# Seven-product form for the last batch and the state reads, with weight sums and early state reads moved, in a fused attention and feed-forward kernel

## The chip, the cores and the metric

The kernel runs on one core of one Trainium2 chip. The metric is the device time of one execution in microseconds (us). "PE" is the matmul engine, "DVE" the vector engine, "ACT" the scalar engine, "POOL" the general engine, "SP" the engine that here only issues DMAs.

## The reference, cut to what matters

```python
# x (8, 8, 512, 64), state (8, 8, 32, 64): batch, head, token, width
scores = scale * x @ state.T ;  a  = softmax(scores)  ; xread = a  @ state   # 512 rows a batch
scores2 = scale * state @ x.T ; a2 = softmax(scores2) ; sread = a2 @ x      # 32 rows a batch
X = concat([xread, sread], tokens), heads side by side    # (8 * 544, 512)
h = X @ w_in                                               # 512 -> 2048
g = s * relu(h)**2 + b
out = g @ w_out                                            # 2048 -> 512
```

The last matrix product (mm2) is what the change rewrites. The 32 state-read rows of all eight batches are collected and treated as one block of 256 tokens, named `sr`, at the very end.

## The kernel before

Weights and activations are fp16, sums fp32. In step s of the main loop the kernel makes the hidden values of batch s (`mm1_x`, 16 pieces f of 128 hidden units) and, between them, the mm2 of batch s-1. For batches 1 to 6 mm2 is the seven-product form of a 2x2 block product (Strassen's idea in Winograd's form): 7 products of quarter size instead of 8, paid for by sums of token blocks (`token_sum`) and of weight blocks (`weight_sums`) on DVE, and by evictions that add partial results. Batches 0 and 7 and `sr` use the plain form:

```python
def mm2_part(key, rr, f0, f1):           # plain: 128 tokens x 512 outputs, 16 matmuls of 512 columns
    ...
def mm2_halves(key, rr):                 # the last 128 tokens of batch 7: two halves of 256 columns
    for n0 in (0, DM // 2):
        ops = psO.tile([P, DM // 2], FP32, tag="o", ...)      # a PSUM bank of its own for each half
        for f in range(NKF):
            mm(ops, G[key, f][:, P * rr : P * rr + P], wof(f)[:, n0:n1], ...)
        evac(ops, key, rr, n0, n1, [(nc.sync, 0, P, x_dst(key, rr)[:, n0:n1])])

# fast_items(b): seven products in banks A (p1, p2), B (p6, p7, p4), C (p5, p3);
# every bank holds two token blocks [P, 2, 256]; 112 matmuls of 256 columns
```

The parts of the main loop that the change touches, and the end:

```python
if s in fast:                            # fast = batches 1 to 6
    if f in (7, 11):
        with tc.issue_after(G["last"]): token_sum(s, 3, f // 8)
    if f in (11, 12, 13): token_sum(s, (1, 2, 4)[f - 11], 0)
    ...
if (s == 1 and f in (5, 7, 9, 14)) or (s == 2 and f in (2, 3, 4, 6)):
    with tc.issue_after(G["last"]): sums.pop(0)()       # one of eight weight sums
# in step 2: state reads of batches 0, 1 and 2, one after the other
at(10, lambda: att_V(s)); at(11, lambda: att_srT(s))
at(12, lambda: att_V(0)); at(12, lambda: att_V(1))
at(13, lambda: att_srT(0)); at(13, lambda: att_srT(1))
...
for f in range(4, NKF):                  # the end
    mm1_sr(f)
    if todo: unit(todo.pop(0))           # batch 7, plain form
for u in todo + sr_units: unit(u)        # sr, plain form; stores on POOL
mm2_halves(last_b, SCH - 1)              # stores on SP
```

PE, SP and POOL run in the order written; the order of DVE and ACT is chosen by the scheduler that builds the program. Output buffers (`osb`) come from a ring of three.

The softmax here doesn't subtract the row's maximum and nothing guards it: scores larger than these inputs give would overflow.

## Time and profile before

| | before |
|---|---|
| time, median of 4 runs | 220.55 us (220.32 to 220.77) |
| span of the profiled run | 218.9 us |
| PE's last matmul ends | 215.2 us |
| last store issued | 215.8 us |

The first line is from the busy table of the page (busy us, share, number of instructions), the second the shares by engine of the chain of work that ended last.

```profile
PE 207.2 (95%) x1916; PEld 125.9 (58%) x1916; DVE 145.3 (66%) x261; ACT 131.6 (60%) x224; POOL 41.5 (19%) x72
...
PE 73%; DVE 13%; DMA 8%; ACT 2%; POOL 1%; issue 1%; SPq 0%
```

PE is the bound: to gain time one must take matmuls away, or waits of PE. A matmul of 512 columns shows as 379 ns busy and one of 256 as 273, but these ends overlap: the starts lie 216 and 109 ns apart, and those are the costs to count with. PE's waits between 48 and 83 us of the kernel before (who waited for whom: total us, times, longest):

```profile
PE srT L68 <- DVE sr L293: 1.0, 2, 0.8
PE oB L68 <- DVE u L477: 0.6, 1, 0.6
PE oA L68 <- DVE osb L372: 0.5, 1, 0.5
PE oA L68 <- DVE qa L474: 0.3, 1, 0.3
PE oB L68 <- DVE s L429: 0.2, 1, 0.2
```

This view counts from the modelled end of a matmul. Counted from start to start, less the distance that the same matmuls keep elsewhere (216 ns after one of 512 columns, 109 after one of 256), the same waits are 1.32, 0.75, 0.58, 0.47 and 0.32 us: 3.4 us, all for DVE. The timeline of DVE just then (start, us, engine, line, operation, out and in) shows why:

```profile
49.49 0.69 DVE L330 TENSOR_TENSOR g<-r 128x1024 f16<-128x1024 f16 x1 [0.32 <-ACT r L324]
50.09 0.69 DVE L423 TENSOR_TENSOR s<-g 128x1024 f16<-128x1024 f16 x1
50.70 0.69 DVE L427 TENSOR_TENSOR s<-g,g 128x1024 f16<-128x1024 f16 x1
51.30 0.75 DVE L372 SCALAR_TENSOR_TENSOR osb<-o,s_bc,bias_bc 128x512 f32<-128x512 f32 x1
51.96 0.68 DVE L429 TENSOR_TENSOR s<-s,g 128x1024 f16<-128x1024 f16 x1
```

No idle time stands in brackets after the first line: DVE is full, one instruction each 0.60 to 0.66 us, and the eviction `osb` that PE waits for stands behind two token sums. Just before, there was room. A window of the same trace, 38 to 49 us (length, then busy us of PE, PEld, DVE, ACT, POOL): DVE worked 6.13 us of 11.

```profile
38.00:49.00 11.00, 11.00 (x93) 4.48 (x92) 6.13 (x12) 8.83 (x16) 2.54 (x4) 1.00 0.95 170
```

The end of the kernel before, from the timeline:

```profile
211.57 3.66 PE L68 MATMUL o<-wo,g 128*128 128x256 f16 x32
...
213.52 0.49 DVE L372 SCALAR_TENSOR_TENSOR osb<-o,s_bc,bias_bc 128x256 f32<-128x256 f32 x1 [0.99 <-PE o L68]
214.03 2.11 SPq L374 DMA_DIRECT2D out_dram<-osb  x2
215.26 0.48 DVE L372 SCALAR_TENSOR_TENSOR osb<-o,s_bc,bias_bc 128x256 f32<-128x256 f32 x1 [1.26 <-PE o L68]
```

This is a good end: the last eviction 0.03 us after PE, and the last store issued at 215.77, 0.54 us after PE's end. From PE's end to the end of the span it takes 3.7 us.

### The profile page before, as it was taken

The page shows a single profiled execution, that of the slowest core. Times are in us where ns is not written, and L with a number is a line of the kernel's source. Part 1 is how long each engine was busy: PE and PEld are TensorE (multiplying, and loading weights), DVE is VectorE, ACT ScalarE, POOL GpSimd, SP SyncE. Part 2 cuts the span into 40 slices and gives each one's busy share as a digit, 9 for nine tenths or more (in the row PEclk, how much of TensorE's full clock was granted, in tenths as well). Part 3 has the DMA queues.
Part 4 walks back from the last instruction along what each step waited for, and adds up shares of the span by engine and source line. Part 5 has one row for each costly group of instructions (what it writes and reads, how often), then busy time and mean ns, then how long its engine had stood idle before and what let it go on. Part 6 is the DMA issues. An engine that isn't in the chain of part 4 may idle for free.

```text
span 218.9 us, 4633 instructions
## 1 busy us (share of the span) xinstructions
PE 207.2 (95%) x1916; PEld 125.9 (58%) x1916; DVE 145.3 (66%) x261; ACT 131.6 (60%) x224; POOL 41.5 (19%) x72
## 2 busy tenths in 40 slices
PE   7897989999989999999999999999999999999993
PEld 2423333345556566667656765676667677655552
DVE  1686737739997778569856985699569955522221
ACT  3685654789488537965697569746974555332200
POOL 5960010403010310212021201120111011120042
PEclk9999999999999999999999999999999999999999
DMA  6999995999901890991199119211311111121123
GB/s 187 220 205 203 206 190 98 137 204 154 143 12 39 185 195 10 167 171 48 48 126 208 58 49 165 78 48 51 96 51 48 51 48 48 51 96 48 51 48 96
DMA packets 38776, 23.72 MB, mean 108 GB/s; under 512 B 24100, under 2 KB 36644, under 8 KB 38756
## 3 DMA queue, kind: packets, MB, share of 16 engines
q0 software_dynamic: 15792, 16.72, 39.4%
q1 hardware_dynamic: 22548, 6.62, 17.3%
q8 instruction: 15, 0.25, 0.5%
q10 hardware_dynamic: 416, 0.10, 0.2%
q14 instruction: 5, 0.04, 0.1%
HBM read 17.33 MB, written 8.91 MB: 120 GB/s over the span
## 4 chain that ended last, share of the span: by engine, by line
PE 73%; DVE 13%; DMA 8%; ACT 2%; POOL 1%; issue 1%; SPq 0%
PE h L68 18%; PE oB L68 14%; PE o L68 11%; PE oC L68 9%; PE oA L68 7%; DMA xn<-in_x_dram 5%; PE Mps L68 4%; PE h_sr L68 3%; PE o_sr L68 3%; DVE g L330 3%; DMA xf<-in_x_dram 3%; DVE s L429 1%; DVE s L427 1%; PE D L68 1%; DVE osb L464 1%; PE V L68 1%
## 5 line engine op out<-in xcount | busy, mean ns | idle before, releaser
L324 ACT ACTIVATE r<-h 128x512 f16<-128x512 f32 x126 | 74.1, 599 | 53.0 <-PE h L68 51.2
L68 PE MATMUL h<-a,M 128*128 128x512 f16 x256 | 74.9, 379 | 1.2 <-DVE a L242 0.7
L330 DVE TENSOR_TENSOR g<-r 128x1024 f16<-128x1024 f16 x64 | 44.2, 691 | 22.1 <-ACT r L324 21.9
L68 PEld LDWEIGHTS <-g 128*128 128x128 f16 x432 | 40.9, 98 | 22.4 <-issue 4.3
L68 PEld LDWEIGHTS <-s 128*128 128x128 f16 x384 | 36.0, 98 | 17.2 <-issue 4.6
L466 POOL DMA_DIRECT2D out_dram<-osb x24 | 16.2, 675 | 119.1 <-DVE osb L464 110.2
L68 PE MATMUL o<-wo,g 128*128 128x512 f16 (+1 forms) x144 | 32.3, 356 | 0.0
L68 PEld LDWEIGHTS <-M 128*128 128x128 f16 x256 | 24.6, 98 | 10.5 <-issue 2.5
L68 PE MATMUL oB<-wd,s 128*128 128x256 f16 x192 | 27.9, 273 | 1.0 <-DVE u L477 0.6
L68 PE MATMUL oA<-wo,g 128*128 128x256 f16 x192 | 27.2, 272 | 0.8 <-DVE osb L372 0.5
L266 ACT CAST M<-Mps 128x1024 f16<-128x1024 f32 x26 | 26.3, 1011 | 0.6
L68 PE MATMUL Mps<-wi,stT 64*32 64x512 f16 x256 | 13.3, 385 | 1.2 <-DMA wi<-in_moe_w_in_dram 1.2
L68 PE MATMUL oC<-wd,s 128*128 128x256 f16 x96 | 14.3, 273 | 0.0
L68 PEld LDWEIGHTS <-stT 64*32 64x32 f16 x384 | 5.3, 90 | 14.7 <-issue 10.3
L68 PE MATMUL oB<-wd,g 128*128 128x256 f16 x96 | 13.6, 273 | 0.0
L68 PE MATMUL oC<-wo,s 128*128 128x256 f16 x96 | 13.4, 273 | 0.0
L324 ACT ACTIVATE r_sr<-h_sr 128x256 f16<-128x256 f32 x16 | 6.1, 382 | 10.7 <-PE h_sr L68 10.7
L242 DVE TENSOR_TENSOR a<-E,R 128x1024 f16<-128x1024 f16 (+1 forms) x9 | 5.7, 632 | 7.2 <-ACT R L241 7.2
L464 DVE SCALAR_TENSOR_TENSOR osb<-oC,s_bc,u 128x512 f32<-128x512 f32 x12 | 9.0, 748 | 2.0 <-PE oC L68 2.0
L240 ACT ACTIVATE L<-D 128x1024 f32<-128x1024 f32 (+1 forms) x9 | 8.3, 925 | 2.5 <-PE D L68 2.5
L217 ACT ACTIVATE E<-T 128x512 f16<-128x512 f32 x16 | 9.4, 596 | 0.7 <-PE T L68 0.7
L330 DVE TENSOR_TENSOR g_sr<-r_sr 128x512 f16<-128x512 f16 x8 | 3.4, 424 | 9.5 <-ACT r_sr L324 9.5
(80 smaller groups left out, 201.8 us busy)
## 6 DMA issues: line engine op xcount, KB each, us to landing
out_dram<-osb POOLq DMA_DIRECT2D x31, 256.0 KB, 2.5
xn<-in_x_dram POOLq DMA_DIRECT2D x7, 512.0 KB, 9.5
wi<-in_moe_w_in_dram POOLq DMA_DIRECT2D x4, 512.0 KB, 9.0
wo<-in_moe_w_out_dram POOLq DMA_DIRECT2D x4, 512.0 KB, 16.2
xf<-in_x_dram SPq DMA_DIRECT2D x2, 512.0 KB, 4.9
out_dram<-osb_sr POOLq DMA_DIRECT2D x8, 64.0 KB, 2.0
out_dram<-osb SPq DMA_DIRECT2D x2, 128.0 KB
st<-in_state_dram POOLq DMA_DIRECT2D x1, 192.0 KB, 19.6
```

The source lines that it names most:

```text
L68: return nc.tensor.matmul(out, lhsT, rhs, start=start, stop=stop, tile_position=tp, is_transpose=is_transpose, skip_group_check=True,)
L217: nc.scalar.activation(a["E"][:, g, :].rearrange("p (m t) -> p m t", m=2), T[:, :, 256 * i : 256 * i + 256], AF.Exp, scale=scale, accum_ou ...
L240: nc.scalar.activation(a["L"][:, sl], Dps, AF.Ln)
L242: nc.vector.tensor_mul(a["a4"][:, sl], a["E"][:, sl], a["R"][:, sl])
L266: nc.scalar.copy(dst, ps)
L324: nc.scalar.activation(r16[:, f % 2], hps, AF.Relu)
L330: nc.vector.tensor_mul(gt[:, f % 4 - 1 : f % 4 + 1], r16, r16)
L427: nc.vector.tensor_add(o, a21, a22)
L429: nc.vector.tensor_sub(o, SQ[b, 1, j], a11)
L464: nc.vector.scalar_tensor_tensor(osb, acc[bank], s_bc, add, ALU.mult, ALU.add)
L466: nc.gpsimd.dma_start(dst[j][:, :, n0 : n0 + NH], osb)
```

## The change

Its intent: save matmul columns in batch 7 and `sr` by the seven-product form as well, and take DVE work out of the crowded stretch. To keep the tail short, the last product of batch 7 is run one token block after the other, each evicted and stored by itself. The core of the diff, cut:

```diff
     def put(bank, add, j, n0):
-        osb = opool.tile([P, 2, NH], FP32, ..., tag="osb")
+        osb = opool.tile([P, ni, NH], FP32, ..., tag="osb")        # ni = 1 for "sr", else 2
         nc.vector.scalar_tensor_tensor(osb, acc[bank], s_bc, add, ALU.mult, ALU.add)
+        if b == "sr":
+            for i in range(4):
+                dst = out_BSn[4 * j + i, S:ST, n0 : n0 + NH]
+                nc.sync.dma_start(dst, osb[Ns * i : Ns * i + Ns, 0])   # 32 rows each
+            return
         ...
+    def put_last(i):                                               # last product of batch 7, block i
+        osb = opool.tile([P, NH], FP32, ..., tag="osb")
+        nc.vector.scalar_tensor_tensor(osb, acc["C"][:, i], s_bc, kept["u2"][:, i], ...)
+        nc.sync.dma_start(dst[0][i][:, NH:DM], osb)
 ...
+    if b == last_b: out += [(3, k, i) for i in range(ni) for k in range(8)]   # block by block
+    else:           out += [(3, k, i) for k in range(8) for i in range(ni)]
 ...
-    if f in (7, 11):
+    if f in ((7, 9) if s == 1 else (7, 11)):
         with tc.issue_after(G["last"]): token_sum(s, 3, f // 8)
+    if s == 1 and f in (12, 13, 14):
+        with tc.issue_after(G["last"]): token_sum(s, (1, 2, 4)[f - 12], 0)
 ...
-    if (s == 1 and f in (5, 7, 9, 14)) or (s == 2 and f in (2, 3, 4, 6)):
+    if (s == 1 and 4 <= f < 11) or (s == 2 and f == 4):            # weight sums
 ...
+    at(13, lambda: att_V(0))                                       # in step 1
+    at(1, lambda: att_srT(0)); at(8, lambda: att_V(1)); at(10, lambda: att_srT(1))   # in step 2
-    at(12, lambda: att_V(0)); at(12, lambda: att_V(1)); at(13, ...); at(13, ...)
 ...                                                               # the end
+    for f in range(4, NKF):
+        mm1_sr(f)
+        ...token sums of "sr"...
+        go(rest, 5)                      # batch 7's products; from f = 12 on also 2 of sr's
+    go(rest, 12); go(rows, 4); go(rest, 8); go(rows, 44)
+    go(rest, 16)                         # last product of batch 7
```

(`tc.issue_after(G["last"])` ties the place of a sum in DVE's order to a matmul; `at(f, ...)` puts a piece of work into step s behind piece f; `V` is the product that makes a batch's state reads, `srT` their transposition on PE. PSUM is the memory in which matmuls add up, in banks; a tile is a buffer that the program asks for.) The state reads use banks of other PSUM pools for A, B and C; their partial results take a free buffer of the inputs.

More of the change, by code (lines that the diff above doesn't have):

```diff
@@ L418, in token_sum @@
     def token_sum(b, i, j):
-        SQ[b, i, j] = spool.tile([P, 4, TH], FP16, name=f"s{i}_{b}_{j}", tag="s")
+        n = (B * Ns if b == "sr" else S) // 2
+        SQ[b, i, j] = spool.tile([P, 4, n], FP16, name=f"s{i}_{b}_{j}", tag="s")
         o = SQ[b, i, j]
-        a11, a21 = G4[b, j][:, :, 0:TH], G4[b, j][:, :, TH:S]
+        a11, a21 = G4[b, j][:, :, 0:n], G4[b, j][:, :, n:]
         if i == 3:
@@ L424, in token_sum @@
             return
-        a12, a22 = G4[b, 2 + j][:, :, 0:TH], G4[b, 2 + j][:, :, TH:S]
+        a12, a22 = G4[b, 2 + j][:, :, 0:n], G4[b, 2 + j][:, :, n:]
         if i == 1:
@@ L435, in fast_items @@
         kept = {}
+        th = (B * Ns if b == "sr" else S) // 2
+        ni = th // P
+        own = xpool.tile([P, 4, NH], FP32, name="u_sr", tag="xn", bufs=5) if b == "sr" else None
         def lhs(p, k, i):
@@ L443, in lhs @@
             if p == 4:
-                return G[b, 8 + k][:, TH + c : TH + c + P]
+                return G[b, 8 + k][:, th + c : th + c + P]
             si = {3: 4, 5: 1, 6: 2, 7: 3}[p]
@@ L458, in keep @@
         def keep(name):
-            kept[name] = upool.tile([P, 2, NH], FP32, name=f"{name}_{b}", tag=name)
+            if b == "sr":
+                i = len(kept)
+                kept[name] = own[:, i : i + 1]
+            else:
+                kept[name] = upool.tile([P, 2, NH], FP32, name=f"{name}_{b}", tag=name)
             return kept[name]
         def put(bank, add, j, n0):
-            osb = opool.tile([P, 2, NH], FP32, name=f"osb_{b}_{j}_{n0}", tag="osb")
+            osb = opool.tile([P, ni, NH], FP32, name=f"osb_{b}_{j}_{n0}", tag="osb")
             nc.vector.scalar_tensor_tensor(osb, acc[bank], s_bc, add, ALU.mult, ALU.add)
+            if b == "sr":
+                for i in range(4):
+                    dst = out_BSn[4 * j + i, S:ST, n0 : n0 + NH]
+                    nc.sync.dma_start(dst, osb[Ns * i : Ns * i + Ns, 0])
+                return
             dst = out_BSn[b, 0:S].rearrange("(q ci cj) n -> cj q ci n", ci=2, cj=2)
             nc.gpsimd.dma_start(dst[j][:, :, n0 : n0 + NH], osb)
+        def put_last(i):
+            osb = opool.tile([P, NH], FP32, name=f"osb_{b}_last_{i}", tag="osb")
+            nc.vector.scalar_tensor_tensor(
+                osb, acc["C"][:, i], s_bc, kept["u2"][:, i], ALU.mult, ALU.add
+            )
+            dst = out_BSn[b, 0:S].rearrange("(q ci cj) n -> cj ci q n", ci=2, cj=2)
+            nc.sync.dma_start(dst[0][i][:, NH:DM], osb)
         def blk(n0):
-            return bias_bc[:, n0 : n0 + NH].unsqueeze(1).broadcast_to([P, 2, NH])
+            return bias_bc[:, n0 : n0 + NH].unsqueeze(1).broadcast_to([P, ni, NH])
         def done(p):
@@ L484, in done @@
                 put("C", kept["u3"], 1, NH)
-                d = bias_d.unsqueeze(1).broadcast_to([P, 2, NH])
+                d = bias_d.unsqueeze(1).broadcast_to([P, ni, NH])
                 nc.vector.tensor_add(keep("qb"), kept["qa"], d)
@@ L495, in item @@
             if fresh and k == 0 and i == 0:
-                acc[bank] = psO.tile([P, 2, NH], FP32, tag="o", name=f"o{bank}_{b}")
+                pool, tag = psO, "o"
+                if b == "sr":
+                    pool, tag = (psH, "h") if bank == "C" else (psA, "att")
+                acc[bank] = pool.tile([P, ni, NH], FP32, tag=tag, name=f"o{bank}_{b}")
             mm(
@@ L503, in item @@
             )
-            if k == 7 and i == 1:
+            if p == 3 and b == last_b:
+                if k == 7:
+                    put_last(i)
+            elif k == 7 and i == ni - 1:
                 done(p)
         order = [(1, 0, 8), (6, 0, 4), (2, 0, 3), (6, 4, 8), (2, 3, 8), (7, 0, 8)]
-        order += [(5, 0, 8), (4, 0, 8), (3, 0, 8)]
-        return [
-            lambda p=p, k=k, i=i: item(p, k, i)
-            for p, k0, k1 in order
-            for k in range(k0, k1)
-            for i in range(2)
-        ]
-    def mm2_halves(key, rr):
-        for n0 in (0, DM // 2):
-            n1 = n0 + DM // 2
-            ops = psO.tile([P, DM // 2], FP32, tag="o", name=f"o_{key}_{rr}_{n0}")
-            for f in range(NKF):
-                mm(
-                    ops,
-                    G[key, f][:, P * rr : P * rr + P],
-                    wof(f)[:, n0:n1],
-                    start=(f == 0),
-                    stop=(f == NKF - 1),
-                )
-            evac(ops, key, rr, n0, n1, [(nc.sync, 0, P, x_dst(key, rr)[:, n0:n1])])
+        order += [(5, 0, 8), (4, 0, 8)]
+        if b == "sr":
+            order = [(p, 0, 8) for p in (1, 6, 2, 7, 5, 4)]
+        out = [(p, k, i) for p, k0, k1 in order for k in range(k0, k1) for i in range(ni)]
+        if b == last_b:
+            out += [(3, k, i) for i in range(ni) for k in range(8)]
+        else:
+            out += [(3, k, i) for k in range(8) for i in range(ni)]
+        return [lambda a=a: item(*a) for a in out]
     def bias_sum():
@@ L569 @@
     units = []
-    for b in (0, B - 1):
-        for i in range(NKF):
-            rr, part = divmod(i, 4)
-            if b == 0:
-                rr, part = 2 * (i // 8) + i % 2, i % 8 // 2
-            units.append((b, rr, part))
-    sr_units = [("sr", rr, part) for rr in range(B * Ns // P) for part in range(4)]
+    for i in range(NKF):
+        units.append((0, 2 * (i // 8) + i % 2, i % 8 // 2))
     last_b = B - 1
-    tail = [u for u in units if u[0] == last_b and u[1] == SCH - 1]
-    units = [u for u in units if u not in tail]
     def unit(u):
@@ L716, in pieces @@
                 at(8, lambda: att_M(nb, 2, "act"))
+            if s == 2:
+                at(1, lambda: att_srT(0))
+                at(8, lambda: att_V(1))
+                at(10, lambda: att_srT(1))
             at(10, lambda: att_V(s))
@@ L720, in pieces @@
                 at(10, lambda: att_M(nb, 3, "act"))
-            if s == 2:
-                at(12, lambda: att_V(0))
-                at(12, lambda: att_V(1))
-                at(13, lambda: att_srT(0))
-                at(13, lambda: att_srT(1))
             if s == last_b:
@@ L731 @@
         sums = weight_sums()
-        fast = range(1, B - 1)
+        fast = range(1, B)
         coming = {}
@@ L752 @@
                 if s in fast:
-                    if f in (7, 11):
+                    if f in ((7, 9) if s == 1 else (7, 11)):
                         with tc.issue_after(G["last"]):
                             token_sum(s, 3, f // 8)
-                    if f in (11, 12, 13):
+                    if s == 1 and f in (12, 13, 14):
+                        with tc.issue_after(G["last"]):
+                            token_sum(s, (1, 2, 4)[f - 12], 0)
+                    if s > 1 and f in (11, 12, 13):
                         token_sum(s, (1, 2, 4)[f - 11], 0)
@@ L767, with go @@
                     fn()
-                if s == last_b and f in (14, 15):
-                    unit(todo.pop(0))
+        token_sum(last_b, 4, 1)
+        rest = coming[last_b][16:]
+        rows = fast_items("sr")
+        def go(items, n):
+            for _ in range(n):
+                items.pop(0)()
         for f in range(4, NKF):
             mm1_sr(f)
-            if todo:
-                unit(todo.pop(0))
-        for u in todo + sr_units:
-            unit(u)
-        mm2_halves(last_b, SCH - 1)
+            if f in (5, 9):
+                token_sum("sr", 3, f // 8)
+            if f in (11, 12, 13):
+                token_sum("sr", (1, 2, 4)[f - 11], 0)
+            if f == 15:
+                for i in (1, 2, 4):
+                    token_sum("sr", i, 1)
+            go(rest, 5)
+            if f >= 12:
+                go(rows, 2)
+        go(rest, 12)
+        go(rows, 4)
+        go(rest, 8)
+        go(rows, 44)
+        go(rest, 16)
 _INS = ['x', 'state', 'moe_w_in', 'moe_w_out', 'moe_s', 'moe_b']
```

## The prediction

> **What bounds the kernel now.** PE: 95% busy (busy table), clock 1.0, 73% of the chain that ended last. In the trace 128x512 matmuls start every 216 ns and 128x256 every 109 ns; the Trainium skill ("TensorE: Matmul & The Clock Gate", "Wait — 56ns, not 53.3ns?") gives 215.7 ns for N=512, and this trace agrees. From 82 us to the end the timeline shows almost no PE gap except 0.46 us at 171.7. What is lost after the start-up lies at 51 to 77 us, where PE waits for DVE, an in-order queue then full without a pause: 0.52 us (oA for osb), 0.47 (oA for qa), 0.32 (oB for s), 0.75 (oB for u), 1.0+0.15 (srT for sr): 3.2 us. From 38 to 49 us DVE idles about 5 us.
>
> **What the change does.**
> 1. Batch 7: 48 matmuls of 512 and 32 of 256 columns (10.37 + 3.50 = 13.87 us) become 112 of 256 (12.24 us): -1.6 us.
> 2. State reads: 32 of 512 (6.91 us) become 56 of 256 (6.12 us): -0.8 us. Both are on PE's critical path: -2.4 us.
> 3. Added DVE work in batch 7 and the tail (8 sums of 0.6 us, 8 of about 0.35 us, evictions) fits: DVE is 20 to 50% busy in the last fifth. The 0.46 us wait stays.
> 4. Seven of eight weight sums (0.6 us each) go into batch 1's idle stretch instead of three; the second token difference goes earlier; evictions of batch 0 come ahead of the sums. V and srT of batches 0 and 1 are spread. I expect 2.7 of the 3.2 us back.
> 5. In the state reads only 8 matmuls (0.87 us) run between two products of one bank; drain, eviction of 128x256 (0.48 us) and handshakes take about as long: +0.15 us.
> 6. The tail. The state reads' results leave as 16 DMAs of 32 rows on SP, ahead of the last two stores on that queue. SP took 0.37 to 0.39 us to issue a 128-row store and 0.23 to 0.36 us for a one-element load; I estimate 0.3 to 0.4 us each, 1.2 to 1.6 us for four, while products finish every 0.87 us. SP falls behind, and with three output buffers the last two evictions wait for stores to land (about 1.5 us after issue). Before, the last store was issued 0.54 us after PE's end; I expect 1.0 to 2.5 us: +1.0 us.
>
> Sum: 220.5 - 2.4 - 2.7 + 0.15 + 1.0 = 216.6 us, -1.8%. Range 215.0 to 218.2. Chances: faster by over 2% 0.38, within 2% 0.61, slower 0.01.
>
> **What would show it.** (1, 2) matmul starts still 109 ns apart; from the last batch's first mm1 to PE's last matmul 2.2 to 2.5 us shorter. (4) PE waits at 48 to 80 us fall from 3.2 to under 0.8 us; DVE's idle time at 38 to 49 us shrinks by about 3 us. (5) PE waits of 0.05 to 0.2 us for DVE in its last 8 us. (6) SP issues DMAs without pause over the last 4 to 6 us; the last osb starts clearly more than 0.1 us after PE's last matmul, released by a DMA; from PE's end to the span's end more than the 3.7 us of before.
>
> **What would make it wrong.** If a 32-row store costs SP under 0.2 us, the tail loses nothing and 215.6 us results. If the scheduler orders DVE in batches 1 and 2 otherwise than I read, half of the 3.2 us stays. If the state reads' sums come late, PE waits up to 1 us more before its products.

## The result, and the profile after

| | before | after |
|---|---|---|
| time, median of 4 runs | 220.55 us | 218.63 us (218.55 to 219.03) |
| ratio after / before | | 0.9917 (0.9900 to 0.9934) |
| span of the profiled run | 218.9 us | 217.0 us |
| PE's last matmul ends | 215.2 us | 212.7 us |
| last store issued | 215.8 us | 214.2 us |

A ratio here is the mean time of one kernel's fast runs over the mean of the other's fast runs of the same rounds, so it is not quite the ratio of the medians quoted beside it. The change is 0.8% faster; 1.8% was predicted, and 218.63 us lies above the predicted range.

The same two lines of the page after:

```profile
PE 205.5 (95%) x1972; PEld 132.1 (61%) x1972; DVE 157.9 (73%) x287; ACT 131.6 (61%) x224; POOL 37.6 (17%) x64
...
PE 72%; DVE 11%; DMA 9%; ACT 3%; SPq 2%; POOL 1%; issue 1%; DVEq 0%
```

PE still bounds the kernel, but SP, which issues DMAs, has come onto the chain with 2%. PE's waits from 36 to 83 us of the kernel after:

```profile
PE o L68 <- DVE osb L372: 0.4, 1, 0.4
PE oB L68 <- DVE u L498: 0.4, 1, 0.4
```

Counted by starts there are 0.46 us (`o` for `osb`, at 38.6 us, new), 0.31 us (`oB` for `s`, at 57.9; not listed by this view) and 0.52 us (`oB` for `u`, at 61.8): 1.3 of the former 3.4 us are left. DVE's work did move into the idle stretch, 9.01 us busy in the same window where it had 6.13:

```profile
38.00:49.00 11.00, 10.61 (x91) 4.34 (x90) 9.01 (x16) 8.38 (x14) 2.18 (x4) 1.00 0.97 169
```

The end after, from the timeline, which is where the time went:

```profile
208.53 5.06 SPq L476 DMA_DIRECT2D out_dram<-osb_sr  x11
...
209.16 1.04 PE L68 MATMUL oC<-wo,s 128*128 128x256 f16 x8
209.36 0.48 DVE L472 SCALAR_TENSOR_TENSOR osb_sr<-oC_sr,s_bc,u_sr 128x256 f32<-128x256 f32 x1 [0.37 <-PE oC_sr L68]
211.15 0.48 DVE L483 SCALAR_TENSOR_TENSOR osb_last<-oC,s_bc,u 128x256 f32<-128x256 f32 x1 [1.30 <-DMA out_dram<-osb_sr]
211.69 1.03 PE L68 MATMUL oC<-wo,s 128*128 128x256 f16 x8 [1.49 <-DVE osb_last L483]
...
213.06 0.48 DVE L483 SCALAR_TENSOR_TENSOR osb_last<-oC,s_bc,u 128x256 f32<-128x256 f32 x1 [1.43 <-DMA out_dram<-osb_sr]
213.69 0.84 SPq L487 DMA_DIRECT2D out_dram<-osb_last  x2
```

Three things are to be seen. SP issues without a pause: 11 stores in 5.06 us, 0.46 us each. The two evictions `osb_last` wait for a DMA, that is for stores of the state reads to land and free one of three buffers. And PE stands still for 1.49 us (1.66 by starts) in the middle of the last product, because it waits for the eviction of the first token block: both blocks are one PSUM tile, which lies in one bank. The Trainium skill ("PSUM — Partial Sum Buffer", "PSUM bank collisions raise a hardware error") says to guard PSUM by bank, not by address, as a matmul and a vector read on one bank collide even at disjoint columns; the trace agrees in so far as the built program waits, here 1.49 us, where the two halves of before, two tiles in two banks, had no gap. It does not show that the bank is the reason: in a run below the two blocks lie in two banks of one tile, and PE still waits, 1.9 us. In the kernel before, POOL issued the state reads' stores and a half had its own bank, so none of the three could be seen there.

From PE's end to the end of the span it now takes 4.3 us instead of 3.7.

### The profile page after: what moved, and what is told of

Same layout as the page of the kernel before. It is cut to its first block, busy times and chain, and to the rows that moved or that the text cites. A ratio compares the mean times of both kernels' runs of the same rounds, so it can differ in the third digit from the quotient of the medians.

```text
span 217.0 us, 4789 instructions
## 1 busy us (share of the span) xinstructions
PE 205.5 (95%) x1972; PEld 132.1 (61%) x1972; DVE 157.9 (73%) x287; ACT 131.6 (61%) x224; POOL 37.6 (17%) x64
## 4 chain that ended last, share of the span: by engine, by line
PE 72%; DVE 11%; DMA 9%; ACT 3%; SPq 2%; POOL 1%; issue 1%; DVEq 0%
PE h L68 19%; PE oB L68 16%; PE oC L68 10%; PE oA L68 9%; DMA xn<-in_x_dram 6%; PE o L68 5%; PE Mps L68 4%; PE h_sr L68 3%; DVE g L330 3%; DMA xf<-in_x_dram 3%; SPq L476 1%; PE D L68 1%; DVE s L430 1%; PE T L68 1%; DVE s L428 1%; DVE osb L472 1%
## 5 line engine op out<-in xcount | busy, mean ns | idle before, releaser
L68 PEld LDWEIGHTS <-s 128*128 128x128 f16 x448 | 42.5, 98 | 19.6 <-issue 5.8
L68 PEld LDWEIGHTS <-g 128*128 128x128 f16 x400 | 37.7, 98 | 18.5 <-issue 3.7
L479 POOL DMA_DIRECT2D out_dram<-osb x27 | 18.3, 677 | 131.6 <-DVE osb L472 125.2
L68 PE MATMUL oB<-wd,s 128*128 128x256 f16 x224 | 32.9, 273 | 0.8 <-DVE u L498 0.4
L68 PE MATMUL oA<-wo,g 128*128 128x256 f16 x224 | 31.7, 273 | 0.1
L68 PE MATMUL oC<-wo,s 128*128 128x256 f16 x112 | 15.5, 272 | 1.5 <-DVE osb_last L483 1.5
L68 PE MATMUL oC<-wd,s 128*128 128x256 f16 x112 | 16.9, 273 | 0.0
L68 PE MATMUL o<-wo,g 128*128 128x512 f16 x64 | 16.3, 380 | 0.4 <-DVE osb L372 0.4
L68 PE MATMUL oB<-wd,g 128*128 128x256 f16 x112 | 15.6, 273 | 0.0
L430 DVE TENSOR_TENSOR s<-s,g 128x1024 f16<-128x1024 f16 x14 | 9.6, 686 | 0.2
```

Of the source, the lines that this page charges most:

```text
L68: return nc.tensor.matmul(out, lhsT, rhs, start=start, stop=stop, tile_position=tp, is_transpose=is_transpose, skip_group_check=True,)
L430: nc.vector.tensor_sub(o, SQ[b, 1, j], a11)
L479: nc.gpsimd.dma_start(dst[j][:, :, n0 : n0 + NH], osb)
```

## The experiments

The theory, called Q in the expectations: SP's queue is the floor of the tail. Sixteen stores at 0.465 us take 7.4 us from the first at 206.3 us, and the last two stores stand behind them; buffers are held until stores land; the shared bank (rather, the shared tile) turns that into a PE wait. Its rivals: B, the shared bank of the two token blocks is the cost; R, too few output buffers are; S, the tail cost little and the shortfall lies in the early batches. Each group of runs below shared a chip and its runs of the kernel before; the changed kernel itself was not run again with them, so compare ratios with its 0.9917. A ratio is known to about 0.0015, or 0.3 us, so two of them tell differences from about 0.5 us on.

### One store for each block of the state reads

```diff
-                for i in range(4):
-                    dst = out_BSn[4 * j + i, S:ST, n0 : n0 + NH]
-                    nc.sync.dma_start(dst, osb[Ns * i : Ns * i + Ns, 0])
+                dst = out_BSn[4 * j : 4 * j + 4, S:ST, n0 : n0 + NH]
+                nc.sync.dma_start(dst, osb[:, 0])
```

> The changed kernel with each of the four result blocks of the state reads stored by one 128-row DMA on SP instead of four of 32 rows. Theory Q (SP's queue is the floor: 16 stores at 0.465 us from 206.3 us on, then the last two behind them, and the output buffers are held until they land): the four stores cost about 0.4 us each, the last two evictions no longer wait for a landing, and the PE wait in the last product falls from 1.49 us to about 0.65 us (it keeps the wait for the eviction of the first token block, as both blocks share one PSUM bank); last store 0.55 us after PE's end; 217.2 us, 1.4 us less than the changed kernel. Rival B (the two token blocks of the last product share one bank, and that alone costs the time): the PE wait stays near 1.5 us and the time within 0.5 us of 218.6.

Measured: 219.41 us, ratio 0.9939 (0.9924 to 0.9954). A miss: not the 1.4 us won, but no gain at all, and by the ratio 0.5 us lost, which is just within the noise. The profiled execution is of no use here (one of six executions took 1161 us, with matmuls far apart on PE throughout; the other five 218.6 to 219.6; what happened in that one is not explained). The run below with the same stores has a fast profile and shows the reason.

### The last two evictions to buffers of their own

```diff
-            osb = opool.tile([P, NH], FP32, name=f"osb_{b}_last_{i}", tag="osb")
+            osb = xpool.tile([P, NH], FP32, name=f"osb_{b}_last_{i}", tag="xn", bufs=5)
```

(A ring of six buffers instead of three did not fit in memory.)

> The changed kernel with the last two evictions writing to buffers of their own, so that they wait for no store to land; the 16 small stores stay. Theory Q: the PE wait falls to about 0.65 us, but the last two stores still stand behind the 16 on SP, so the last one is issued at about 214.2 us as before and the time stays within 0.3 us of 218.6. Rival R (too few output buffers is the cause): the time falls by the 0.85 us that PE no longer waits, to 217.8 us or below.

Measured: 218.69 us, ratio 0.9921. As Q said, against R: the wait of PE fell to 0.6 us, and the time did not move. The view of the tile `osb_last` of this run (starts of the evictions and stores; what DVE idled for; who waited):

```profile
L483 DVE SCALAR_TENSOR_TENSOR osb_last<-oC,s_bc,u x2: 483/484/484, 209.8 to 211.4; 128x256 f32<-128x256 f32 x2
L487 SPq DMA_DIRECT2D out_dram<-osb_last x2: 367/372/378, 213.3 to 213.7; - x2
its engine sat idle before it (us, times) until:
  PE oC L68: 1.5, 2
who waited for it (us, times):
  PE oC L68: 0.6, 1
```

The evictions no longer wait for a DMA and are done by 211.9 us, but their stores are issued at 213.3 and 213.7: the results wait their turn in SP's queue for 3.0 and 1.8 us.

### Two banks for the last product, as one tile

```diff
+                if b == last_b and bank == "C":
+                    acc[bank] = att_ps([P, 2, 512], FP32, f"oC_{b}")[:, :, 0:NH]
+                elif b == "sr" and bank in "AB":          # to make room: A and B in one tile
+                    acc[bank] = acc["AB"][:, n : n + 1, 0:NH]
```

> The changed kernel with the two token blocks of the last product of batch 7 in two PSUM banks; the 16 small stores stay. Theory Q: PE's wait of 1.49 us disappears and PE ends near 211.1 us instead of 212.7, but the evictions wait for the landings and the stores for SP's queue as before: time within 0.3 us of 218.6. Rival B: 1.5 us less, 217.1 us.

Measured: 220.28 us, ratio 0.9987, 0.7% slower than the change. The experiment failed in its making: a tile over two banks is still treated as one, so the wait in the last product did not go (1.9 us in the next run, which has the same tiles and a fast profile), and A and B of the state reads, now in one tile, waited for each other. So what PE waits on here is the tile, as the program guards it. (Its profiled execution was slow, 267 us at a granted clock of 0.754; the four fast runs count.)

### Both of these

> Both of the above: one store for each block of the state reads, and two banks. Theory Q: PE does not wait in its last 5 us by more than 0.2 us, the last store is issued about 0.55 us after PE's end, and the whole loss in the tail is gone: 216.1 us, 2.5 us less than the changed kernel and about 1.1 us less than one store alone. If the products themselves had saved less than the 2.4 us counted from matmul starts, it would stay above 217 us.

Measured: 220.52 us, ratio 0.9994. The waits of PE of this run over the whole span:

```profile
PE oC L68 <- DVE osb_last L482: 1.9, 1, 1.9
...
PE oAB_sr L68 <- DVE u_sr L497: 0.8, 1, 0.8
...
PE oAB_sr L68 <- DVE osb_sr L472: 0.6, 1, 0.6
```

The second and third are the new waits of the shared tile. The first is still the last product, and longer, because `osb_last` waited 3.1 us for stores of the state reads. Two of these, issued at 209.80 and 210.67 us, released it only at 213.12 and 214.98, that is 3.3 and 4.3 us later, where the stores of 32 rows took 1.6 us. The Trainium skill ("DMA: Bandwidth & Descriptors", "Why a DMA increments its semaphore by 16 and not by 1") says that the number of DMA engines is the largest up to 16 that divides the slowest dimension of both sides; here the output's is 4 batches, so four engines. The trace agrees: the semaphore of each of these four stores was updated four times at the landing (and once about 1 us after the issue), that of every 32-row store of the changed kernel 16 times. So fewer, larger stores in this shape trade issue time for landing time.

### Small stores on two queues

```diff
-                    nc.sync.dma_start(dst, osb[Ns * i : Ns * i + Ns, 0])
+                    eng = nc.scalar if i % 2 else nc.sync
+                    eng.dma_start(dst, osb[Ns * i : Ns * i + Ns, 0])
```

> The changed kernel with the 16 small stores of the state reads going alternately to SP and ACT (8 each), the last two stores on SP as before. The store as one DMA had failed as a test: it spread over four rows groups only and landed late. Theory Q: two queues halve the backlog, SP is done with the small stores near 210 us, the last two evictions no longer wait for a landing, PE's wait in the last product falls from 1.49 to about 0.65 us (the shared bank remains), the last store is issued about 0.55 us after PE's end; 217.2 us, 1.4 less than the changed kernel. Rival B (the shared bank alone): PE's wait stays at 1.5 us, time within 0.4 us of 218.6.

Measured: 217.35 us, ratio 0.9859; the change had 0.9917, so 1.3 us are won (0.0058 of 220.4). As Q said to 0.2 us. PE's wait in the last product is 0.8 us (one of the two evictions still waited 0.6 us for a landing, which Q had not expected), and the last store is issued 0.55 us after PE's end (212.77 and 212.22 us), as before the change.

### Two separate tiles for the last product

```diff
+                if b == last_b and bank == "C":
+                    acc["C0"] = psO.tile([P, 1, NH], FP32, tag="o", name="oC0_last")
+                    acc["C1"] = psH.tile([P, 1, NH], FP32, tag="h", name="oC1_last")
```

(The eviction of product 5 of batch 7 then is two instructions.)

> The changed kernel with the two token blocks of the last batch's bank C as two separate PSUM tiles (the earlier try, one tile over two banks, was still treated as one and made new waits); the 16 small stores stay on SP. Theory Q: PE's wait in the last product is gone (under 0.2 us), PE ends about 1.5 us earlier, but the last eviction waits for the same landing and the last store for the same queue: time within 0.3 us of 218.6. Rival B: 217.1 us.

Measured: 219.16 us, ratio 0.9942 (0.9929 to 0.9956): B is refuted. PE's wait in the last product is gone and PE ends at 211.3 us, 1.4 us earlier, but the time is no better, by the ratio 0.5 us worse. Q had said no change within 0.3 us. The view of `osb_last`:

```profile
L489 DVE SCALAR_TENSOR_TENSOR osb_last<-oC_last,s_bc,u x2: 484/484/484, 211.4 to 213.4; 128x256 f32<-128x256 f32 x2
L493 SPq DMA_DIRECT2D out_dram<-osb_last x2: 368/372/377, 214.0 to 214.5; - x2
its engine sat idle before it (us, times) until:
  DMA out_dram<-osb_sr: 2.8, 2
who waited for it (us, times):
```

Nobody waits for the evictions, but they still wait for landings, and the last store leaves at 214.5, 3.2 us after PE. About 0.3 us of the loss show in the same queue: the second result of the state reads was evicted at 207.97 instead of 207.61 us, after a wait for a buffer held by a store of batch 7, SP paused from 207.98 to 208.49, and the last store left 0.3 us later than in the changed kernel. This comes with the eviction in two instructions: that store of batch 7 was issued at 204.41 instead of 204.07 us and landed at 207.85 instead of 206.65.

### Two queues and two tiles

> Both. Theory Q: no PE wait over 0.2 us in the last 5 us, last store about 0.55 us after PE's end, 216.2 us, 2.4 us less than the changed kernel: the whole saving of the seven-product form at last visible. It should beat both kernels by more than any single part.

Measured: 217.28 us, ratio 0.9860, no better than two queues alone: a miss of 1.1 us. `osb_last` waited 1.3 us for landings, two evictions of the state reads before it 0.9 and 0.5 us for landings of batch 7's stores, and the last store left 1.0 us after PE's end. With queue and bank free, the three buffers bind.

### The last product not by token block

```diff
-        if b == last_b:
-            out += [(3, k, i) for i in range(ni) for k in range(8)]
-        else:
-            out += [(3, k, i) for k in range(8) for i in range(ni)]
+        out += [(3, k, i) for k in range(8) for i in range(ni)]
```

(With one eviction and one store on SP for both blocks.)

> The changed kernel with the last product in the order of the other batches (both token blocks together, one eviction of 128x512 and one 256 KB store on SP), the 16 small stores on SP as before. Theory Q: PE's wait is gone, but the store stands behind the 16 on SP, so it is issued at about 213.7 us instead of 214.2: 218.2 us, 0.4 less. Rival B (the order by token block is what costs): 1.5 us less, 217.1 us.

Measured: 219.43 us, ratio 0.9952, 0.8 us slower than the change. PE ends at 211.2 us, 1.5 us earlier, and the store is issued at 213.80, right behind the queue, as Q said; B is refuted a second time. Instead of 0.4 us better it is worse, for which the trace gives a part only: issuing the large store took 0.65 us, and SP's wait for its landing ended at 216.4 us, 0.3 us later than for the last store of the change. The rest is open.

### The three parts of the change, each alone

`products_only` is the changed kernel with weight sums, token sums and V/srT where they were; `sums_only` and `slots_only` are the kernel before with one of the two moves. Their diffs are those above.

> The changed kernel without its other two parts: weight sums, token sums and V/srT of batches 0 and 1 stand as in the kernel before; seven products for batch 7 and the state reads, last product by token block. Theory Q: 2.4 us of matmul starts are saved, and the tail gives them back (1.66 us PE wait, 0.6 us later last store, 0.2 us before a qa): within 0.5 us of the kernel before, 220.1 to 221.0. Rival S (the shortfall lies in the early batches, and the products gained most of their 2.4 us): 218.5 to 219.

Measured: 221.09 us, ratio 1.0030 (1.0017 to 1.0043). The seven-product form, as the change wrote it, cost 0.3% rather than saving 1.1%. S is refuted. PE's wait in the last product is there, as in the changed kernel (after 83 us; from the waits of PE):

```profile
PE oC L68 <- DVE osb_last L483: 1.6, 1, 1.6
```

> The kernel before with only the move of the weight sums and token sums of batch 1. By the PE waits of the two traces (0.52, 0.47, 0.32, 0.75 us before; 0.39, 0.31, 0.52 us after) it gains 0.8 us: 219.7. Rival S2: the gain that the prediction counted, 1.6 us: 218.9.

Measured: 219.66 us, ratio 0.9969: 0.7 us.

> The kernel before with only V and srT of batches 0 and 1 spread. The waits of srT for sr (1.0 and 0.15 us) vanish: 1.1 us less, 219.4. If the extra evictions in the full stretch of DVE at 54 to 60 us hold PE, less: 219.8.

Measured: 219.19 us, ratio 0.9947: 1.2 us. Both as the trace's waits had it. Alone, the spread state reads also lengthen two other waits, since their evictions came into the crowded stretch; that of `oA` for `osb` falls from 0.5 to 0.2 us. From `products_only` to the changed kernel, which adds both moves, the ratio falls from 1.0030 to 0.9917, 2.5 us, more than 0.7 and 1.2. By the traces, PE reaches the wait for `s` in step 7 0.7 us earlier with the one move, 1.1 with the other and 2.15 with both, so the two are worth some 0.3 us more together; the rest is within the noise. (PE's waits from 34 to 83 us of that run; before, these two were 0.6 and 0.3):

```profile
PE oB L68 <- DVE u L477: 0.7, 1, 0.7
PE oA L68 <- DVE qa L474: 0.6, 1, 0.6
```

### Queue, bank and buffers together

Small stores on SP and ACT in turn, two tiles for the last product, the last two results and two of the four results of the state reads in buffers of the input ring:

```diff
+            if b == "sr" and bank != "B" and (j, n0) != (0, NH):
+                osb = xpool.tile([P, ni, NH], FP32, name=f"osb_{b}_{j}_{n0}", tag="xn", bufs=5)
```

> The changed kernel with small stores on SP and ACT in turn, two PSUM tiles for the last product's token blocks, and separate buffers for two of the state reads' results and the last two results. With queues and banks alone 217.3 was measured, as two evictions still waited about 0.9 us for a landing. Theory Q (queue, bank and buffers bind in turn, and with all three free only matmul starts are left): no PE wait over 0.25 us in the last 8 us, last store 0.55 us after PE's end, 216.3 to 216.6. If landing waits were not what held 217.3, the time stays there.

Measured: 216.26 us, ratio 0.9813 (0.9799 to 0.9826), 2.3 us better than the change. Its end, from the timeline:

```profile
208.91 1.91 PE L68 MATMUL oC_last<-wo,s 128*128 128x256 f16 x16
...
210.65 1.08 SPq L497 DMA_DIRECT2D out_dram<-osb_last  x2
210.86 0.48 DVE L493 SCALAR_TENSOR_TENSOR osb_last<-oC_last,s_bc,u 128x256 f32<-128x256 f32 x1 [0.39 <-PE oC_last L68]
```

The 16 matmuls of the last product run without a gap, the last eviction starts 0.04 us after PE's end (210.82) and the last store is issued at 211.37, 0.55 us after it. The end of the kernel before is restored, and the saving of the products is there. Two queues with free buffers but one tile were not run, so what the second tile adds once the others are free is not shown. Nor were the small stores put on POOL, which had issued the state reads' stores before the change (8 of them, 0.50 us each).

### The order of DVE's work in batches 1 and 2

On that kernel, the first four weight sums one step later (two of the eight now at f = 8) and the last one two steps later:

```diff
-                if (s == 1 and 4 <= f < 11) or (s == 2 and f == 4):
+                if (s == 1 and 5 <= f < 11) or (s == 2 and f == 6):
                     with tc.issue_after(G["last"]):
-                        sums.pop(0)()
+                        for _ in range(2 if (s, f) == (1, 8) else 1):
+                            sums.pop(0)()
```

> On the kernel with the freed tail (216.3 us): the first weight sum one step later, behind the evictions of batch 0, and the last one two steps later, behind the eviction u that PE waits for. If the order on DVE makes these waits, the wait of o for osb (0.39 us) goes and that of oB for u falls from 0.36 to below 0.1 us: 0.75 us less, 215.5. If the batch's own sums make them: the waits stay, within 0.2 us of 216.3.

Measured: 215.46 us, ratio 0.9776 (0.9763 to 0.9790), 0.8 us better, as expected; this is the best version found, 2.2% faster than the kernel before. Both waits are gone. Why they existed is seen in DVE's order in the changed kernel:

```profile
37.02 0.74 DVE L564 TENSOR_SCALAR bias_bc<-bias_ps,b_bc 128x512 f32<-128x512 f32 x1
37.68 0.68 DVE L414 TENSOR_TENSOR wd<-wo 128x1024 f16<-128x1024 f16 x1
38.28 1.40 DVE L372 SCALAR_TENSOR_TENSOR osb<-o,s_bc,bias_bc 128x512 f32<-128x512 f32 x2
...
60.89 0.68 DVE L414 TENSOR_TENSOR wd<-wo,wd 128x1024 f16<-128x1024 f16 x1
61.49 0.75 DVE L498 SCALAR_TENSOR_TENSOR u<-oB,s_bc,qa 128x512 f32<-128x512 f32 x1
```

Each time a weight sum `wd` stands right before an eviction that PE's next matmul waits for (at 38.28 us the first of two). In the kernel before, no sum stood before the first, and in this run it is so again:

```profile
37.92 1.41 DVE L372 SCALAR_TENSOR_TENSOR osb<-o,s_bc,bias_bc 128x512 f32<-128x512 f32 x2
```

> The same with V and srT of batch 0 five steps earlier, in DVE's idle time, so that their evictions (0.4 and 0.2 us) no longer stand before the sum that oB waits for at 57.9 us. If the order on DVE makes it: that wait (0.31 us) goes too, 215.2. If not: as the run before.

(V of batch 0 at f = 8 and srT at f = 10 of step 1.) Measured: 216.46 us, ratio 0.9824: a miss. PE's waits from 34 to 83 us:

```profile
PE srT L68 <- ACT M L266: 1.0, 1, 1.0
PE oB L68 <- DVE s L430: 0.2, 1, 0.2
```

The transposition `srT` now waits for an ACT eviction to free its PSUM buffer, a new wait of 1.0 us, and the gap before the sum `s` stayed (0.32 us by starts). So V and srT of batch 0 do not make that gap; what would remove it is open.

## Why the prediction was wrong, point by point

| term | predicted us | measured us | from |
|---|---|---|---|
| products (1, 2) | -2.4 | -2.33 | starts, see below |
| early waits (4) | -2.7 | -2.15 | waits by starts, 3.4 to 1.3 |
| bank turns (5) | +0.15 | +0.09 | starts at 205.5 us |
| wait of oA for qa | 0 | +0.23 | starts at 190.4 us, new |
| tail (6) | +1.0 | +2.28 | PE wait 1.66, PE's end to span's end +0.63 |
| sum | -3.95 | -1.9 | span 218.9 to 217.0 |

Points 1 and 2 were right. From the matmul that waits for `s` in step 7 (it stands behind the same work in both kernels, at 171.66 and 169.52 us) to the start of PE's last matmul it took 43.29 us before and 42.93 after, of which 1.66, 0.23 and 0.09 us are new waits: 40.96 us of matmuls, 2.33 less. The Trainium skill's 215.7 ns between matmuls of 512 columns ("TensorE: Matmul & The Clock Gate", "Wait — 56ns, not 53.3ns?") agrees with the 216 ns counted here.

Point 3 was right in its main claim: the 0.46 us wait stayed (0.45) and DVE kept up. It missed one small thing: in step 7 a token sum stands before the eviction `qa`, and PE waits 0.23 us.

Point 4 had the mechanism right and the size wrong. DVE's idle time at 38 to 49 us shrank by 2.9 us, as written, and the evictions of batch 0 at 51 us came ahead of the sums. But the prediction did not ask what the first moved weight sum would push back, and that is where the new 0.46 us came from; nor did it see that the last weight sum stayed right before `u`. `sums_after_stores` shows that these two cost 0.8 us. The two moves alone brought 0.7 and 1.2 us.

Point 6 is the step that failed: "SP falls behind, and with three output buffers the last two evictions wait for stores to land ... +1.0 us". The direction and both waits were as predicted, the size was 2.3 us, by the spans and by what `free_buffers` won back, for two reasons. First, the issue of a 32-row store was taken as 0.3 to 0.4 us; it was 0.34 to 0.42, and 0.465 from start to start, so 16 took 7.4 us. Second, a wait was not seen at all: with both token blocks of the last product in one tile, the late eviction of the first block stops PE, 1.66 us. The +1.0 us counted only how late the last store would be. Freeing the bank alone (two tiles: no better) or the buffers alone (no change) left the time where the queue held it; two queues won 1.3 us, and only all three the 2.3.

What stays open: whether one bank with two tiles would wait as well, what the second tile adds to two queues and free buffers, the 0.31 us before the sum `s` in step 2, a part of the loss of `last_whole`, and the single execution of 1161 us.

## What to carry to other kernels

When a product is split so that its results leave in more and smaller stores, count the issue time of the stores on their queue against the pace at which results come: here a queue slower than the results (four stores in about 1.9 us, a result each 0.87 us) moved the whole saving into the tail, and a second queue was worth 1.3 us. At the end of a program, ask for each of the last results which buffer, which PSUM tile and which queue it needs, because here they bound one behind the other, and freeing the buffers or the tile alone gained nothing. When work is moved into the idle time of an in-order engine, look at what stands directly behind it in its new place.

## What the Trainium skill lacked or had wrong

- "DMA: Bandwidth & Descriptors" ("Issuing engines are not separate DMA queues") says that issuing from several engines only saves the sequencer's time, "usually small relative to the DMA itself", and gives no figure there (rough ones stand in the page's table on trn3, for "previous generations", and in "SBUF — State Buffer"), nor does it warn of many stores in a row. Here SP needed 0.34 to 0.42 us for a store of 32 rows of 1 KB, 0.465 us from one to the next, against 1.6 us from issue to landing; with 16 in a row it was 7.4 us, and spreading them over SP and ACT won 1.3 us.
- The same page does not set the issue time of a store of 128 rows beside one of 32: SP took 0.37 us for the one and up to 0.42 for the other, so four of 32 rows cost SP about four times one of 128; it took 0.54 to 0.67 us for one with rows in 4 x 32 shape and 0.65 us for 256 KB.
- "PSUM — Partial Sum Buffer" gives the rule of one engine at a time per bank, but no cost: with the eviction free to start at once, the turn from one half of a tile in one bank to the other cost PE 0.6 us here (0.74 by starts, `osb_apart`), and nothing with two tiles in two banks (`own_banks`). One tile over two banks still waited (1.9 us, `one_store_two_banks`), so the bank's own share is not shown.
